# First loads on two queues, and GpSimd's start-up work in another order

## The chip, the cores and the metric

The kernel runs on one core of one Trainium2 chip. The metric is device time in microseconds (us) for one execution, the median of several runs. A profile of one further execution shows each engine's instructions: PE (TensorE matmul), PEld (its weight loads), DVE (VectorE), ACT (ScalarE), POOL (GpSimd) and SP (SyncE, which here only issues transfers). SPq, ACTq and so on are the engines' sequencers.

## What is computed

Linear attention with random features, and behind it a mixture of eight experts, each token going to one of them. Cut to what matters:

```python
q_s, k_s = q * D ** -0.25, k * D ** -0.25          # (8, 8, 576, 64) each
phi = lambda x: exp(h - max(h)) / sqrt(128)        # h = x @ omega.T - sum(x * x) / 2, omega is (128, 64)
q_p, k_p = phi(q_s), phi(k_s)
kv, z = einsum('bhsm,bhsd->bhmd', k_p, v), k_p.sum(axis=2)
x = (q_p @ kv) / (q_p @ z + 1e-6)                  # heads joined: 4608 rows of 512
logits = x @ w_gate                                # 8 experts
e = argmax(logits)                                 # gate weight: softmax(logits)[e]
out = gate * (relu(x @ w1[e]) @ w2[e])             # w1: 512 x 1024, w2: 1024 x 512
```

## The kernel before

**Units.** Attention is worked through in 72 units, nine for each of the eight batches: unit -1 takes the last 64 positions of all eight heads (the remainder), units 0 to 7 take 512 positions of one head. `run` walks over them as a software pipeline. In step i, PE turns the inputs of unit i+1 (`tr`, in PSUM) and DVE copies them to `th` (L157); PE multiplies `th` of unit i by the scaled omega (`pp`, L166) and DVE takes the maxima (`mx`, L172); ACT takes the exponentials `kp` of unit i and `qp` of unit i-1 (L180, four instructions each). Behind them come the turn of `qp`, the sums over `v` (`kf`, L206) and the outputs. `pp` has two PSUM buffers, so the product of a unit waits until the exponentials of the unit two before it are done. `tr`, `pt_om` and the turned `qp` share one PSUM buffer of tag "tt".

**Loads.** `load(b)` issues a batch's transfers: the remainders of k and q into `kqr` (two halves each, L111), the heads of k, q and v (L115), and the remainder of v into the zeroed buffers `rv` (two halves, L111). Batch 0 starts with single heads of k and q (128 KB), then come the gate weights into `G` (L124, two halves), then v for two heads, the remainder of v, and pairs of heads (256 KB each). All are issued by SP, in this order. Two copies of omega are loaded ahead of them (L75); PE turns them (L77) and ACT scales the result into `omt` (L79), which every `pp` needs.

**Counters.** The transfers that SP and ACT issue are counted on eight semaphores in turn (DMAHW0 to DMAHW7 in the rows of the built program). A transfer is issued only when the earlier ones on its semaphore have landed; that wait stands in the issuing engine's instruction stream. The recording layer sets each engine's order from the order of the code; between engines it decides which transfer comes next on the eight semaphores.

**Start-up.** GpSimd makes the identity, clears the gather buffers `xg` and `xgm` (L789), makes the routing's constants (`Routing.setup`, L406 to L454; DVE turns some of them into other types, L420 and L450 to L454), copies the identity into `G` (L89, 16 copies) and clears the four `rv` buffers (L95). The experts' phase follows attention and is not touched.

Of the kernel before, what the change touches and what calls it, by code (L numbers as in the profile page):

```python
# [8 lines left out]
F32 = mybir.dt.float32  # L9
F32R = mybir.dt.float32r  # L10
BF16 = mybir.dt.bfloat16
I32 = mybir.dt.int32
# [45 lines left out]
class Attention:  # L58
    def __init__(self, tc, ctx, ps, io, q, k, v, omega, wg, xs, routing, ident):
        self.tc, self.nc = tc, tc.nc  # L60
        self.q, self.k, self.v, self.xs, self.routing, self.ident = q, k, v, xs, routing, ident
        nc = tc.nc
        pool = lambda n, b, **kw: ctx.enter_context(tc.tile_pool(name=n, bufs=b, **kw))
        self.cp = pool("at_c", 1)
        self.io, self.ps = io, ps
        self.open = ExitStack()
        self.pp = self.open.enter_context(tc.tile_pool(name="ps_a", bufs=2, space=PSUM))
        self.tt = self.open.enter_context(tc.tile_pool(name="ps_t", bufs=1, space=PSUM))
        self.wk = pool("at_wk", 2)
        self.xo = pool("at_x", 2)  # L70
        cp = self.cp

        om = self.wk.tile([P, 2, D], F32, name="om", tag="kp")
        for i in range(2):
            nc.sync.dma_start(om[:, i, :], omega)  # L75
        pt = self.tt.tile([P, 2, 512], F32, name="pt_om", tag="tt")
        nc.tensor.transpose(pt[:, 0, :P], om.rearrange("p a d -> p (a d)"), ident)  # L77
        self.om = cp.tile([P, M], F32, name="omt")
        nc.scalar.mul(self.om, pt[:, 0, :P], SCALE)  # L79

        self.G = cp.tile([P, H, W - 1], F32, name="G")
        self.one = cp.tile([P, 1], F32, name="one")
        nc.gpsimd.memset(self.one, 1.0)
        self.eps = cp.tile([P, 1], F32, name="eps")
        nc.gpsimd.memset(self.eps, EPS)
        for a in range(2):
            r = slice(a * D, (a + 1) * D)
            for h in range(H):
                nc.gpsimd.tensor_copy(self.G[r, h, :D], ident[r, r])  # L89
        self.wg = wg  # L90


        self.rv = [[cp.tile([P, NP, D], F32, name=f"rv{i}{a}") for a in range(2)] for i in range(2)]
        for t in self.rv[0] + self.rv[1]:
            nc.gpsimd.memset(t, 0.0)  # L95
        self.st, self.last = {}, {}

    def load(self, b):
        nc, io = self.nc, self.io
        s = {}  # L100
        s["kqr"] = io.tile([P, 2, NP, D], F32, name=f"kqr_{b}", tag="kqr")
        for nm in "kq":
            s[nm] = io.tile([P, H, NJ, D], F32, name=f"{nm}_{b}", tag=nm)
        s["v"] = io.tile([P, H, NJ, D], F32, name=f"v_{b}", tag="v")
        s["vr"] = self.rv[b % 2]
        def rest(nms):
            for n, src in nms:
                rem = src[b, :, SM:, :].rearrange("(i a) p d -> a p i d", a=2)
                for a in range(2):
                    to = s["vr"][a] if n == 2 else s["kqr"][:, n]  # L110
                    nc.sync.dma_start(to[a * SR:(a + 1) * SR], rem[a])  # L111

        def main(nms, h):
            for nm, src in nms:
                nc.sync.dma_start(s[nm][:, h], src[b, h, :SM, :].rearrange("h (p j) d -> p h j d", j=NJ))  # L115

        kq, v = (("k", self.k), ("q", self.q)), (("v", self.v),)
        rest(((0, self.k), (1, self.q)))
        if b == 0:
            main(kq, slice(0, 1))  # L120
            main(kq, slice(1, 2))
            for a in range(2):
                with nc.allow_non_contiguous_dma(reason="gate weights"):
                    nc.sync.dma_start(self.G[a * D:(a + 1) * D, :, D:], self.wg.rearrange("(h d) e -> d h e", d=D))  # L124
            main(v, slice(0, 2))
        rest(((2, self.v),))
        for c in range(2 if b == 0 else 0, H, 2):
            main(kq + v, slice(c, c + 2))
        s["kva"] = self.xo.tile([P, H, W], F32, name=f"kva_{b}", tag="kva")
        s["x"] = self.xo.tile([P, NJ, H, D], F32, name=f"x_{b}", tag="x")  # L130
        s["xr"] = self.xo.tile([P, NP, D], F32, name=f"xr_{b}", tag="xr")
        s["lg"] = self.xo.tile([P, NJ, E], F32, name=f"lg_{b}", tag="lg")
        s["lgr"] = self.xo.tile([P, E, NP], F32, name=f"lgr_{b}", tag="lgr")
        self.st[b] = s
# [158 lines left out]
    def run(self, pre):  # L293
# [8 lines left out]
        for i in range(n):  # L302
# [30 lines left out]
                self.routing.row(2 if i % 4 == 0 else 1, self.nc.gpsimd)  # L333
            self.unit_sum(*u)
            pre.ahead(i - n)
            if u1:
                self.next = self.room(f"tr_{i}")
                self.routing.product(self.next[:, 1, 256:])
# [56 lines left out]
class Routing:  # L395
# [8 lines left out]
    def setup(self):  # L404
# [6 lines left out]
        self.RM = t("rt_RM", [P, NG, GT])  # L411
        self.RH = t("rt_RH", [P, NLT, 2, P], BF16)
        self.EX = t("rt_EX", [P, GT, E + 1])
        nc.gpsimd.memset(self.EX[:, :, E:], 1e-9)
        nc.gpsimd.memset(self.CU[:, 0, :], 0.0)

        self.iop = t("rt_iop", [P, P])
        self.iob = t("rt_iob", [P, P], BF16)
        nc.gpsimd.iota(self.iop, pattern=[[1, P]], base=0, channel_multiplier=0, allow_small_or_imprecise_dtypes=True)
        nc.vector.tensor_copy(self.iob, self.iop)  # L420
        self.rev = t("rt_rev", [P, E])
        nc.gpsimd.iota(self.rev, pattern=[[-1, E]], base=E, channel_multiplier=0, allow_small_or_imprecise_dtypes=True)
        self.zero = t("rt_zero", [P, P], BF16)
        nc.gpsimd.memset(self.zero, 0.0)
        self.ones = t("rt_ones", [P, P], BF16)
        nc.gpsimd.memset(self.ones, 1.0)
        self.tri = t("rt_tri", [P, P], BF16)
        nc.gpsimd.affine_select(out=self.tri, in_=self.ones, pattern=[[1, P]], compare_op=ALU.is_gt, fill=0.0,
                                base=0, channel_multiplier=-1)
        self.low = t("rt_low", [P, E, E])  # L430
        self.upp = t("rt_upp", [P, E, E])
        nc.gpsimd.memset(self.low, 1.0)
        nc.gpsimd.memset(self.upp, 1.0)
        nc.gpsimd.affine_select(out=self.low, in_=self.low, pattern=[[1, E], [-1, E]], compare_op=ALU.is_gt, fill=0.0,
                                base=0, channel_multiplier=0)
        nc.gpsimd.affine_select(out=self.upp, in_=self.upp, pattern=[[-1, E], [1, E]], compare_op=ALU.is_gt, fill=0.0,
                                base=0, channel_multiplier=0)
        self.fold = t("rt_fold", [P, SR])
        nc.gpsimd.tensor_copy(self.fold, ident[:, :SR])
        nc.gpsimd.tensor_tensor(out=self.fold, in0=self.fold, in1=ident[:, SR:], op=ALU.add)  # L440
        idi = t("rt_id", [P, NG, GT], I32)
        nc.gpsimd.iota(idi[:, :, :GT - 1], pattern=[[2 * S, NG], [S, 2], [1, NJ]], base=0, channel_multiplier=NJ)
        for a in range(2):
            nc.gpsimd.iota(idi[a * SR:(a + 1) * SR, :, GT - 1:], pattern=[[2 * S, NG]], base=SM + a * S,
                           channel_multiplier=1)
        part = t("rt_part", [P, NLT], I32)
        self.ihi = t("rt_ihi", [P, NLT])
        self.ilo = t("rt_ilo", [P, NLT])
        flat = idi.rearrange("p g s -> p (g s)")
        nc.vector.tensor_single_scalar(part, flat, 6, op=ALU.logical_shift_right)  # L450
        nc.vector.tensor_copy(self.ihi, part)
        nc.vector.tensor_scalar_add(self.ihi, self.ihi, -float(NT // 64))
        nc.vector.tensor_single_scalar(part, flat, 63, op=ALU.bitwise_and)
        nc.vector.tensor_copy(self.ilo, part)  # L454

    def open(self, ps, tag):
        self.ps, self.tag = ps, tag
# [313 lines left out]
class Experts:  # L771
# [6 lines left out]
    def __init__(self, tc, ctx, rt, xs, w1, w2, out, ident, ps):  # L778
# [6 lines left out]
        self.idx0 = cp.tile([P, 2], U32, name="idx0")  # L785
        self.flags = cp.tile([1, 5, NPR + 2], I32, name="flags")
        self.xg = [cp.tile([P, 2, ROW], F32, name=n) for n in ("xg", "xgm")]
        for x in self.xg:
            self.nc.gpsimd.memset(x, 0.0)  # L789
        rt.setup()  # L790
        *rt.after[3], last = rt.head(4, self.idx0, self.flags)
        rt.late[5] = [last]
# [327 lines left out]
def attention_moe(tc, q, k, v, omega, wg, w1, w2, out, xs):  # L1120
    nc = tc.nc
    with ExitStack() as ctx:
        cp = ctx.enter_context(tc.tile_pool(name="cp", bufs=1))
        ps = ctx.enter_context(tc.tile_pool(name="ps", bufs=1, space=PSUM))
        sched = lambda: tc.manual_schedule(engines={ET.PE, ET.Activation, ET.DVE, ET.Pool, ET.SP})
        ident = cp.tile([P, P], F32, name="ident")
        make_identity(nc, ident)
        rt = Routing(tc, ctx, xs, ident)
        ex = Experts(tc, ctx, rt, xs, w1, w2, out, ident, ps)
        with ExitStack() as c2:  # L1130
            io = c2.enter_context(tc.tile_pool(name="at_io", bufs=2))
            at = Attention(tc, c2, ps, io, q, k, v, omega, wg, xs, rt, ident)
            rt.open(ps, "nu")
            with sched():
                at.run(ex)
                ex.rest()
        with ExitStack() as c4:
            with sched():
                ex.run(c4, at.open.close)
# [23 lines left out]
```

## Time and profile before

| | us |
|---|---|
| median of three runs | 698.99 |
| lowest and highest | 698.91, 699.36 |
| the profiled execution, its own time | 701.15 |
| span of the profiled execution, first to last instruction | 699.3 |
| PE busy in the span | 672.8 |
| ACT busy | 359.9 |
| DVE busy | 372.6 |
| GpSimd busy | 272.4 |

The span is the part that the profile sees; 1.85 us of the profiled execution lie around it. Start times in rows count from the start of the span. A row of the timeline merges instructions that follow each other and are alike ("x4"), and a row with an engine's q at its end is an issue of a transfer; the transfer itself lands later, and the list of transfers gives the time from issue to landing. Idle time before an instruction stands in brackets with what ended it.

### The profile page before, as it was taken

To read this page: it belongs to the slowest core of one execution; us is meant where nothing else is said; L and a number is where in the kernel's file an instruction comes from. 1 tells how busy PE (TensorE), PEld (TensorE's weight loads), DVE (VectorE), ACT (ScalarE), POOL (GpSimd) and SP (SyncE) were. 2 spreads that over 40 slices of the span, in tenths; PEclk is the share of its full clock that TensorE was granted. 3 is DMA by queue.
4 is the path that set the end of the run, shared out by engine and by line. 5 is a ranking of instruction groups with operands and counts; after the bars stand their busy time and mean duration, and the time that the engine had idled before them with its cause. 6 is when DMAs were issued, how large, how long until landed. Compare 5 with 4: busy or idle time off the path is not lost. (4 is left out here: it accounts for less than half of the span.)

```text
span 699.3 us, 19723 instructions
## 1 busy us (share of the span) xinstructions
PE 672.8 (96%) x7596; PEld 615.6 (88%) x7596; DVE 372.6 (53%) x738; ACT 359.9 (51%) x1096; POOL 272.4 (39%) x484
## 2 busy tenths in 40 slices
PE   5999999999999999999999999999999999999992
PEld 4999999999898977899899988999898999998891
DVE  4788888888887778532222253422383365422220
ACT  3999999999998944322212262222262263222120
POOL 6455547886887763222112202222231132122020
PEclk9999999999999999999999999999999999999997
DMA  5953836628492124851233247332267338422200
GB/s 160 269 168 114 268 88 191 209 76 252 138 373 73 34 76 138 286 179 64 93 97 108 91 158 241 108 106 71 84 205 242 108 112 320 138 79 61 78 18 21
DMA packets 92432, 99.57 MB, mean 142 GB/s; under 512 B 28943, under 2 KB 72975, under 8 KB 91665
## 3 DMA queue, kind: packets, MB, share of 16 engines
q1 hardware_dynamic: 85744, 78.91, 35.9%
q0 software_dynamic: 6560, 19.03, 8.2%
q8 instruction: 72, 1.18, 0.7%
q14 instruction: 56, 0.45, 0.2%
HBM read 71.06 MB, written 29.51 MB: 144 GB/s over the span
## 5 line engine op out<-in xcount | busy, mean ns | idle before, releaser
L943 PEld LDWEIGHTS p<-xb,w1p 128*128 128x128 f32 x1632 | 198.1, 192 | 1.7 <-issue 0.5
L943 PE MATMUL p<-xb,w1p 128*128 128x256 f32 x1632 | 198.9, 283 | 0.0
L868 PE MATMUL p<-w2p,hh 128*128 128x512 f32 x576 | 177.8, 390 | 0.0
L1014 POOL DMA_INDIRECT out_dram<-ys,idx x38 | 39.4, 1038 | 313.4 <-ACT ys L1013 201.3
L868 PEld LDWEIGHTS p<-w2p,hh 128*128 128x128 f32 x576 | 107.0, 188 | 21.3
L868 PE MATMUL p<-w2p,hl 128*128 128x512 f32 x312 | 117.7, 389 | 0.0
L1013 ACT ACTIVATE ys<-p,gt 128x512 f32<-128x512 f32 x38 | 26.1, 688 | 163.2 <-PE p L868 146.2
L999 DVE SCALAR_TENSOR_TENSOR hl<-p,hh 128x512 fp32r<-128x512 f32 x68 | 46.0, 688 | 80.5 <-ACT hh L995 78.3
L995 ACT ACTIVATE hh<-p 128x512 fp32r<-128x512 f32 x68 | 39.9, 598 | 91.5 <-PE p L943 91.5
L172 DVE TENSOR_REDUCE mx<-pp 128x8 f32<-128x1024 f32 x64 | 78.0, 1218 | 11.4 <-PE pp L166 10.7
L180 ACT ACTIVATE qp<-pp,mx 128x128 f32<-128x128 f32 x256 | 77.4, 438 | 0.0
L180 ACT ACTIVATE kp<-pp,mx 128x128 f32<-128x128 f32 x256 | 74.2, 387 | 4.6 <-DVE de L264 1.1
L166 PE MATMUL pp<-omt,th 64*128 64x128 f32 x1024 | 73.4, 285 | 0.0
L868 PEld LDWEIGHTS p<-w2p,hl 128*128 128x128 f32 x312 | 58.5, 188 | 12.2
L166 PEld LDWEIGHTS pp<-omt,th 64*128 64x128 f32 x1024 | 64.8, 194 | 0.0
L192 POOL TENSOR_TENSOR k<-kp 128x256 f32<-128x256 f32 x64 | 46.6, 728 | 27.7 <-ACT kp L180 21.8
L157 DVE COPY th<-tr 128x512 f32<-128x512 f32 x63 | 43.3, 687 | 6.8 <-PE tr L151 4.8
L927 DVE STREAM_TRANSPOSE xgm<-xq 128x512 f32<-128x512 f32 x18 | 18.9, 1086 | 51.3 <-DMA xq<-pair_rows 51.3
L255 PE MATMUL nu<-kva,qt 128*64 128x73 f32 x1008 | 46.0, 233 | 0.0
L224 ACT COPY qt<-t 128x512 f32<-128x512 f32 x64 | 42.0, 656 | 3.1 <-PE t L151 2.5
L255 PEld LDWEIGHTS nu<-kva,qt 128*64 128x64 f32 x1008 | 36.7, 136 | 4.2
L206 PE MATMUL kf<-kp,v 128*64 128x128 f32 x512 | 39.4, 275 | 0.0
(365 smaller groups left out, 1002.0 us busy)
## 6 DMA issues: line engine op xcount, KB each, us to landing
w1s<-in_moe_w_dram SPq DMA_DIRECT2D x5, 2048.0 KB, 8.8
w2s<-in_moe_w_dram SPq DMA_DIRECT2D x5, 2048.0 KB, 11.0
xq<-pair_rows SPq DMA_DIRECT2D x76, 128.0 KB, 2.9
v<-in_v_dram SPq DMA_DIRECT2D x32, 256.0 KB, 6.4
token_rows<-x SPq DMA_DIRECT2D x8, 1024.0 KB, 8.0
k<-in_k_dram SPq DMA_DIRECT2D x31, 256.0 KB, 5.2
q<-in_q_dram SPq DMA_DIRECT2D x31, 256.0 KB, 5.9
pair_rows<-xg SPq DMA_DIRECT2D x10, 512.0 KB, 2.8
```

The lines of the kernel that those rows point to most:

```text
L157: self.nc.vector.tensor_copy(t.rearrange("p n (a t) -> p a n t", a=2), s[("tr", h)])
L166: nc.tensor.matmul(o[:, a, n, :], t[r, n, :], self.om[r], start=True, stop=True)
L172: self.nc.vector.tensor_reduce(out=mx, in_=s[("pp", h)], axis=AX.X, op=ALU.max, negate=True)
L180: self.nc.scalar.activation(o[:, j, :], p[:, a, 2 * n + i, :], AF.Exp, bias=mx[:, a, 2 * n + i:2 * n + i + 1])
L192: nc.gpsimd.tensor_tensor(out=k2, in0=kp[:, :2, :], in1=kp[:, 2:, :], op=ALU.add)
L206: nc.tensor.matmul(pkv[c * D:(c + 1) * D, :M], vv, kk, start=n < 2, stop=n > 2)
L224: self.nc.scalar.copy(qt.rearrange("p n (a t) -> p a n t", a=2), s[("t2", h)])
L255: nc.tensor.matmul(o[r, j, :], qt[:, j, r], kva[:, h if h >= 0 else 2 * j + a, :], start=True, stop=True)
L868: self.nc.tensor.matmul(p, x, w[:, c, :], start=c == 0 and x is h and w is self.w2h, stop=c == self.NF - 1 and x is l)
L943: return [lambda w=w, x=x, c=c, n=n: self.nc.tensor.matmul(o, w[:, c, f], x[:, c, :], start=n == 0, stop=n == len(ops) - 1) for n, (w, x, ...
L995: self.nc.scalar.activation(a, self.p_1[g], AF.Relu)
L999: self.nc.vector.scalar_tensor_tensor(out=b, in0=self.p_1[g], scalar=0.0, in1=a.bitcast(F32), op0=ALU.max, op1=ALU.subtract)
```

## The change

1. Of the first transfers, ACT now issues one copy of omega, the remainder of q, both halves of the gate weights, the first v and the remainder of v for batch 0. SP issues the rest. PE's turn of omega and ACT's scaling (`scaled`) are called from `load`, behind the issues of `kqr`.
2. GpSimd clears the four `rv` buffers ahead of the copies into `G`.
3. The routing's constants (`Routing.constants`) and the clearing of `xg` and `xgm` (`pre.clear`) are called at the end of step 0 of `run`. Attention is built within the hand-ordered stretch (`sched()`).

```diff
-        for i in range(2):
-            nc.sync.dma_start(om[:, i, :], omega)
-        pt = self.tt.tile([P, 2, 512], F32, name="pt_om", tag="tt")
-        nc.tensor.transpose(pt[:, 0, :P], om.rearrange("p a d -> p (a d)"), ident)
+        for i, eng in enumerate((nc.sync, nc.scalar)):
+            eng.dma_start(om[:, i, :], omega)
         self.om = cp.tile([P, M], F32, name="omt")
-        nc.scalar.mul(self.om, pt[:, 0, :P], SCALE)
+
+        def scaled():
+            pt = self.tt.tile([P, 2, 512], F32, name="pt_om", tag="tt")
+            nc.tensor.transpose(pt[:, 0, :P], om.rearrange("p a d -> p (a d)"), ident)
+            nc.scalar.mul(self.om, pt[:, 0, :P], SCALE)
+        self.scaled = scaled
...
+        for t in self.rv[0] + self.rv[1]:
+            nc.gpsimd.memset(t, 0.0)
         for a in range(2):
             r = slice(a * D, (a + 1) * D)
             for h in range(H):
                 nc.gpsimd.tensor_copy(self.G[r, h, :D], ident[r, r])
...
-                    nc.sync.dma_start(to[a * SR:(a + 1) * SR], rem[a])
+                    (nc.scalar if b == 0 and n else nc.sync).dma_start(to[a * SR:(a + 1) * SR], rem[a])
...
-                nc.sync.dma_start(s[nm][:, h], src[b, h, :SM, :].rearrange("h (p j) d -> p h j d", j=NJ))
+                (nc.scalar if b == 0 and nm == "v" and not h.start else nc.sync).dma_start(s[nm][:, h], src[b, h, :SM, :].rearrange("h (p j) d -> p h j d", j=NJ))
...
         if b == 0:
+            self.scaled()
             main(kq, slice(0, 1))
...
-                    nc.sync.dma_start(self.G[a * D:(a + 1) * D, :, D:], self.wg.rearrange("(h d) e -> d h e", d=D))
+                    nc.scalar.dma_start(self.G[a * D:(a + 1) * D, :, D:], self.wg.rearrange("(h d) e -> d h e", d=D))
...
             pre.ahead(i - n)
+            if i == 0:
+                self.routing.constants()
+                pre.clear()
...
-        for x in self.xg:
-            self.nc.gpsimd.memset(x, 0.0)
+        self.clear = lambda: [self.nc.gpsimd.memset(x, 0.0) for x in self.xg]
...
-            at = Attention(tc, c2, ps, io, q, k, v, omega, wg, xs, rt, ident)
-            rt.open(ps, "nu")
             with sched():
+                at = Attention(tc, c2, ps, io, q, k, v, omega, wg, xs, rt, ident)
+                rt.open(ps, "nu")
```

ACT's instructions at the start, before, with the semaphores that each waits for (`kp_-1` and `qp_-1` are the exponentials of unit -1, `kp_0` those of unit 0):

```order
L79 ACT_TABLE_LOAD
L79 ACTIVATE omt<-pt_om 128x128 [waits PE_49]
L180 ACTIVATE kp_-1_254<-pp_-1_242,mx_-1_251 128x128 [waits DVE_49]
L180 ACTIVATE kp_-1_254<-pp_-1_242,mx_-1_251 128x128 x3
L180 ACTIVATE qp_-1_308<-pp_-1_242,mx_-1_251 128x128 x4
```

And now:

```order
L75 DMA om<-in_omega_dram 128x64
L114 DMA kqr_162<-in_q_dram 64x4x64 x2
L81 ACT_TABLE_LOAD
L81 ACTIVATE omt<-pt_om 128x128 [waits PE_49]
L128 DMA G<-in_moe_w_gate_dram 64x8x8 [waits DMAHW1_49]
L128 DMA G<-in_moe_w_gate_dram 64x8x8 [waits DMAHW3_49]
L118 DMA v_165<-in_v_dram 128x2x256 [waits DMAHW5_49]
L114 DMA rv_138<-in_v_dram 64x4x64 [waits DMAHW7_49,Pool_49]
L114 DMA rv_139<-in_v_dram 64x4x64 [waits DMAHW1_49,Pool_49]
L184 ACTIVATE kp_-1_230<-pp_-1_218,mx_-1_227 128x128 [waits DVE_49]
L184 ACTIVATE kp_-1_230<-pp_-1_218,mx_-1_227 128x128 x3
L184 ACTIVATE qp_-1_308<-pp_-1_218,mx_-1_227 128x128 x4
```

Three issues now stand ahead of the table load, and five, each with a wait for a transfer semaphore, between `omt` and the first exponentials. SP's issues before, from the first head on:

```order
L115 DMA k_190<-in_k_dram 128x256
L115 DMA q_191<-in_q_dram 128x256
L115 DMA k_190<-in_k_dram 128x256 [waits DMAHW0_49]
L115 DMA q_191<-in_q_dram 128x256 [waits DMAHW1_49]
L124 DMA G<-in_moe_w_gate_dram 64x8x8 [waits DMAHW2_49]
L124 DMA G<-in_moe_w_gate_dram 64x8x8 [waits DMAHW3_49]
L115 DMA v_192<-in_v_dram 128x2x256 [waits DMAHW4_49]
L111 DMA rv_179<-in_v_dram 64x4x64 [waits DMAHW5_49,Pool_49]
L111 DMA rv_180<-in_v_dram 64x4x64 [waits DMAHW6_49,Pool_49]
L115 DMA k_190<-in_k_dram 128x2x256 [waits DMAHW7_49]
L115 DMA q_191<-in_q_dram 128x2x256 [waits DMAHW0_49]
```

And now, from the first head on:

```order
L118 DMA k_163<-in_k_dram 128x256
L118 DMA q_164<-in_q_dram 128x256
L118 DMA k_163<-in_k_dram 128x256 [waits DMAHW0_49]
L118 DMA q_164<-in_q_dram 128x256 [waits DMAHW1_49]
L118 DMA k_163<-in_k_dram 128x2x256 [waits DMAHW2_49]
L118 DMA q_164<-in_q_dram 128x2x256 [waits DMAHW3_49]
L118 DMA v_165<-in_v_dram 128x2x256 [waits DMAHW4_49]
L118 DMA k_163<-in_k_dram 128x2x256 [waits DMAHW5_49]
L118 DMA q_164<-in_q_dram 128x2x256 [waits DMAHW6_49]
L118 DMA v_165<-in_v_dram 128x2x256 [waits DMAHW7_49]
L118 DMA k_163<-in_k_dram 128x2x256 [waits DMAHW0_49]
```

The gate weights, the first v and the remainder of v are gone from SP's row, and the pairs of heads follow the single heads at once. DVE's first instructions before:

```order
L420 CAST rt_iob<-rt_iop 128x128
L450 TENSOR_SCALAR rt_part<-rt_id 128x36
L451 CAST rt_ihi<-rt_part 128x36
L452 TENSOR_SCALAR rt_ihi<-rt_ihi 128x36
L453 TENSOR_SCALAR rt_part<-rt_id 128x36
L454 CAST rt_ilo<-rt_part 128x36
L157 COPY th_-1_229<-tr_first 128x2x4x64
L157 COPY th_0_240<-tr_second 128x2x4x64
L172 TENSOR_REDUCE mx_-1_251<-pp_-1_242 128x8
L157 COPY th_1_295<-tr_259 128x2x4x64
```

And now:

```order
L161 COPY th_-1_205<-tr_first 128x2x4x64
L161 COPY th_0_216<-tr_second 128x2x4x64
L176 TENSOR_REDUCE mx_-1_227<-pp_-1_218 128x8
L440 CAST rt_iob<-rt_iop 128x128
L459 TENSOR_SCALAR rt_part<-rt_id 128x36
L460 CAST rt_ihi<-rt_part 128x36
L461 TENSOR_SCALAR rt_ihi<-rt_ihi 128x36
L462 TENSOR_SCALAR rt_part<-rt_id 128x36
L463 CAST rt_ilo<-rt_part 128x36
L161 COPY th_1_295<-tr_259 128x2x4x64
```

The six instructions on the routing's constants now stand between the maxima of unit -1 and the copy of unit 1's turned inputs.

## Rows read from the trace of the kernel before

**Rows 1.** The page, part 1: busy us, share of the span, instructions.

```profile
PE 672.8 (96%) x7596; PEld 615.6 (88%) x7596; DVE 372.6 (53%) x738; ACT 359.9 (51%) x1096; POOL 272.4 (39%) x484
```

**Rows 2.** Busy time of each engine by stretch, granted clock, DMA share, GB/s.

```profile
4.00:8.00 4.00, 1.69 (x10) 0.98 (x10) 1.90 (x7) 0.12 (x1) 3.83 (x23) 1.00 0.66 172
18.00:20.00 2.00, 2.00 (x22) 1.67 (x20) 0.78 (x2) 1.73 (x8) 0.51 (x1) 1.00 1.09 343
20.00:24.00 4.00, 4.00 (x82) 3.82 (x82) 2.59 (x4) 2.97 (x12) 1.61 (x4) 1.00 0.89 200
20.00:240.00 220.00, 216.30 (x4533) 203.50 (x4532) 183.11 (x397) 211.59 (x809) 147.87 (x291) 1.00 0.57 174
```

**Rows 3.** The timeline of PE: start, us, instruction, idle time before it.

```profile
6.70 0.47 PE L151 MATMUL tr_first<-ident,kqr 64*128 64x64 f32 x3 [0.83 <-DMA kqr<-in_q_dram]
...
14.61 0.48 PE L151 MATMUL tr<-ident,q 64*128 64x64 f32 x4 [0.36 <-DMA q<-in_q_dram]
14.88 2.02 PE L166 MATMUL pp<-omt,th 64*128 64x128 f32 x16
```

**Rows 4.** Weight loads of the products L166 in two stretches: duration ns min/median/max.

```profile
L166 PEld LDWEIGHTS pp<-omt,th x32: 330/330/335, 10.6 to 16.3; 64*128 64x128 f32 x32
...
L166 PEld LDWEIGHTS pp<-omt,th x176: 188/188/194, 22.2 to 57.8; 64*128 64x128 f32 x176
```

**Rows 5.** The timeline of SP: start and duration of the issues.

```profile
0.81 0.89 SPq L75 DMA_DIRECT2D om<-in_omega_dram  x2
1.74 1.41 SPq L111 DMA_DIRECT2D kqr<-in_k_dram  x2
3.20 1.27 SPq L111 DMA_DIRECT2D kqr<-in_q_dram  x2
4.51 0.60 SPq L115 DMA_DIRECT2D k<-in_k_dram  x1
...
9.21 1.29 SPq L111 DMA_DIRECT2D rv<-in_v_dram  x2
10.56 0.60 SPq L115 DMA_DIRECT2D k<-in_k_dram  x1
...
14.79 0.53 SPq L115 DMA_DIRECT2D v<-in_v_dram  x1
...
20.84 0.97 SPq L115 DMA_DIRECT2D k<-in_k_dram  x1
22.03 0.37 SPq L115 DMA_DIRECT2D q<-in_q_dram  x1
```

**Rows 6.** Transfers issued at 4.51, 10.56 and 14.79: KB, us from issue to landing.

```profile
k<-in_k_dram SPq DMA_DIRECT2D x1, 128.0 KB, 2.6
...
k<-in_k_dram SPq DMA_DIRECT2D x1, 256.0 KB, 3.1
...
v<-in_v_dram SPq DMA_DIRECT2D x1, 256.0 KB, 7.2
```

**Rows 7.** The timeline of ACT: the table load and the exponentials of unit -1.

```profile
0.81 1.28 ACT L79 ACT_TABLE_LOAD   x1 [0.81 <-PEq L1150]
...
11.77 1.14 ACT L180 ACTIVATE kp_-1_254<-pp_-1_242,mx_-1_251 128x128 f32<-128x128 f32 x4 [7.64 <-DVE mx_-1_251 L172]
12.78 1.16 ACT L180 ACTIVATE qp_-1_308<-pp_-1_242,mx_-1_251 128x128 f32<-128x128 f32 x4
```

**Rows 8.** The timelines of DVE and GpSimd: constants, maxima of unit -1, last clears.

```profile
3.48 0.61 DVE L420 CAST rt_iob<-rt_iop 128x128 bf16<-128x128 f32 x1 [3.48 <-POOL rt_iop L419]
5.42 0.20 DVE L450 TENSOR_SCALAR rt_part<-rt_id 128x36 int32<-128x36 int32 x1 [1.33 <-POOL rt_id L444]
...
6.46 0.18 DVE L454 CAST rt_ilo<-rt_part 128x36 f32<-128x36 int32 x1
...
10.51 1.23 DVE L172 TENSOR_REDUCE mx_-1_251<-pp_-1_242 128x8 f32<-128x1024 f32 x1 [1.13 <-PE pp_-1_242 L166]
...
8.87 1.07 POOL L95 MEMSET rv<- 128x256 f32 x4
```

More of the change, by code (lines that the diff above doesn't have):

```diff
@@ L85, in __init__ @@
         nc.gpsimd.memset(self.eps, EPS)
+        self.wg = wg
+        self.rv = [[cp.tile([P, NP, D], F32, name=f"rv{i}{a}") for a in range(2)] for i in range(2)]
+        for t in self.rv[0] + self.rv[1]:
+            nc.gpsimd.memset(t, 0.0)
         for a in range(2):
@@ L89, in __init__ @@
                 nc.gpsimd.tensor_copy(self.G[r, h, :D], ident[r, r])
[L90 to L95, printed above, removed]
         self.st, self.last = {}, {}
@@ L413, in setup, with constants @@
         self.EX = t("rt_EX", [P, GT, E + 1])
+        self.iop = t("rt_iop", [P, P])
+        self.iob = t("rt_iob", [P, P], BF16)
+        self.rev = t("rt_rev", [P, E])
+        self.zero = t("rt_zero", [P, P], BF16)
+        self.ones = t("rt_ones", [P, P], BF16)
+        self.tri = t("rt_tri", [P, P], BF16)
+        self.low = t("rt_low", [P, E, E])
+        self.upp = t("rt_upp", [P, E, E])
+        self.fold = t("rt_fold", [P, SR])
+        self.idi = t("rt_id", [P, NG, GT], I32)
+        self.part = t("rt_part", [P, NLT], I32)
+        self.ihi = t("rt_ihi", [P, NLT])
+        self.ilo = t("rt_ilo", [P, NLT])
+    def constants(self):
+        nc, ident = self.nc, self.ident
         nc.gpsimd.memset(self.EX[:, :, E:], 1e-9)
         nc.gpsimd.memset(self.CU[:, 0, :], 0.0)
-        self.iop = t("rt_iop", [P, P])
-        self.iob = t("rt_iob", [P, P], BF16)
         nc.gpsimd.iota(self.iop, pattern=[[1, P]], base=0, channel_multiplier=0, allow_small_or_imprecise_dtypes=True)
         nc.vector.tensor_copy(self.iob, self.iop)
-        self.rev = t("rt_rev", [P, E])
         nc.gpsimd.iota(self.rev, pattern=[[-1, E]], base=E, channel_multiplier=0, allow_small_or_imprecise_dtypes=True)
-        self.zero = t("rt_zero", [P, P], BF16)
         nc.gpsimd.memset(self.zero, 0.0)
-        self.ones = t("rt_ones", [P, P], BF16)
         nc.gpsimd.memset(self.ones, 1.0)
-        self.tri = t("rt_tri", [P, P], BF16)
         nc.gpsimd.affine_select(out=self.tri, in_=self.ones, pattern=[[1, P]], compare_op=ALU.is_gt, fill=0.0,
                                 base=0, channel_multiplier=-1)
-        self.low = t("rt_low", [P, E, E])
-        self.upp = t("rt_upp", [P, E, E])
         nc.gpsimd.memset(self.low, 1.0)
@@ L437, in setup @@
                                 base=0, channel_multiplier=0)
-        self.fold = t("rt_fold", [P, SR])
         nc.gpsimd.tensor_copy(self.fold, ident[:, :SR])
         nc.gpsimd.tensor_tensor(out=self.fold, in0=self.fold, in1=ident[:, SR:], op=ALU.add)
-        idi = t("rt_id", [P, NG, GT], I32)
-        nc.gpsimd.iota(idi[:, :, :GT - 1], pattern=[[2 * S, NG], [S, 2], [1, NJ]], base=0, channel_multiplier=NJ)
+        nc.gpsimd.iota(self.idi[:, :, :GT - 1], pattern=[[2 * S, NG], [S, 2], [1, NJ]], base=0, channel_multiplier=NJ)
         for a in range(2):
-            nc.gpsimd.iota(idi[a * SR:(a + 1) * SR, :, GT - 1:], pattern=[[2 * S, NG]], base=SM + a * S,
+            nc.gpsimd.iota(self.idi[a * SR:(a + 1) * SR, :, GT - 1:], pattern=[[2 * S, NG]], base=SM + a * S,
                            channel_multiplier=1)
[L446 to L451, printed above, removed]
+        flat = self.idi.rearrange("p g s -> p (g s)")
+        nc.vector.tensor_single_scalar(self.part, flat, 6, op=ALU.logical_shift_right)
+        nc.vector.tensor_copy(self.ihi, self.part)
         nc.vector.tensor_scalar_add(self.ihi, self.ihi, -float(NT // 64))
-        nc.vector.tensor_single_scalar(part, flat, 63, op=ALU.bitwise_and)
-        nc.vector.tensor_copy(self.ilo, part)
+        nc.vector.tensor_single_scalar(self.part, flat, 63, op=ALU.bitwise_and)
+        nc.vector.tensor_copy(self.ilo, self.part)
     def open(self, ps, tag):
```

## The prediction

> **What bounds the kernel now.** I read the page's part 1 first: PE is busy for 96% of the span [rows 1]. The windows say where it is not. From 20 to 240 us, the rest of attention, PE is busy for 216.3 of 220 us [rows 2], so nearly every microsecond that the start gains or loses is still there at the end. Only the start itself has holes. The mark by which I measure it is the first product that is followed by work without a break, `pp` of unit 1, which starts on PE at 14.88, after a turn that waited for a load of q until 14.61 [rows 3]. A change that moves this product by some time moves the end by the same time, unless something else comes last.
>
> Two levels of PE's clock lie in this stretch. The granted clock reads 1.00 in every window [rows 2], yet the weight loads of the same products take 330 ns up to 16 us and 188 ns from 22 us on [rows 4]: 1.2 GHz first, 2.4 GHz later, and the rise came some 6 us after PE's last wait. I take it that the rise moves with the work. If it comes a microsecond earlier or later than that, half of the PE work in that microsecond is won or lost, 0.5 us at most, and this goes into the range.
>
> **Where the loads stand.** SP issues without a break from 0.81 to about 9 us, then the remainder of v waits for GpSimd's clears, and the pair of heads that PE waits for goes out at 10.56 only [rows 5]. It lands 3.1 us later [rows 6], at 13.7. In the stretch from 4 to 8 us the DMA engines are busy for 0.66 of the time at 172 GB/s, against 343 GB/s from 18 to 20 us [rows 2]: at first the issues are the limit, not the transfers.
>
> **What sharing the queues wins.** SP loses one copy of omega (half of 0.89, so 0.45 us) and the remainder of q (1.27 us and a gap of 0.04) [rows 5]. The first head of k goes out at 4.51 - 1.77 = 2.74 and lands 2.6 us later [rows 6], at 5.34. ACT issues the remainder of q from 1.28 on, where SP issued it from 3.20 on: 1.92 us earlier. The turn of the remainder, whose last part waited for that load and ended at 7.17 [rows 3], would end at 5.25, if the table load is not late. That load now stands behind three issues: 0.81 + 0.45 + 1.31 = 2.57, and 1.28 us of loading [rows 7] end at 3.9, early enough for `omt` at about 4.2. The maxima of unit -1 start at 10.51 [rows 8] and would then start at about 8.7 and end at 9.9.
>
> **What the constants cost.** On DVE they now stand behind these maxima: 0.61 us for the first and 1.22 us from 5.42 to 6.64 for the other five [rows 8], so 1.83 us. They would end at 11.7, the copy of unit 1 at 12.4, and its product could start at 12.85. GpSimd's start-up work, which ended at 9.94 [rows 8], is the same in another order, with the clears of `xg` last; what DVE needs is made by then. If nothing else came last, the product would start 2.0 us earlier than at 14.88. Without DVE's wait for room behind the maxima it would be up to 1.83 us more; so much this step costs in that case, and nothing where PE is held by something later.
>
> **What the moved issues cost.** ACT now issues five transfers between `omt` and the exponentials of unit -1, and each has a wait for one of the eight semaphores in turn. Such a wait is in the rows of before: SP was free at 21.81, yet issued a load of q at 22.03 [rows 5], just after the load of v issued at 14.79 had landed, 7.2 us later, at 22.0 [rows 6]. The two have nothing in common but the semaphore. In the changed program the remainder of v on ACT waits for DMAHW7 to count two loads, and the two before it there are the first q and the third pair of v, the sixth pair of heads on SP. The first v on ACT waits in the same way for the second pair of k. ACT works its row in order, so the exponentials of unit -1 queue behind the landing of a load that is not needed before unit 4.
>
> When does that sixth pair land? From the first k's landing at 5.34, three single heads and six pairs follow, 7.5 pairs in all. In the trace nine pairs in a row landed from 13.66 to 21.99 [rows 5, 6], eight steps of 1.04 us. So 7.5 x 1.04 = 7.8 us, at 13.1. The gate weights and the first v come in between on the other queue; I add 0.3 us for them, an estimate, and take 13.4. The bounds are the rates of two stretches: a pair is 262,144 bytes, 0.76 us at 343 GB/s and 1.31 us at 200 GB/s [rows 2], so 11.1 and 15.2. Then two issues with their waits, 1.29 us on SP [rows 5], and the exponentials of unit -1 start at 14.7 (12.4 to 16.5) instead of 11.77 [rows 7]. No row shows an issue on ACT; on SP one took 0.45 us to 0.97 us [rows 5], so the pair lies between 0.9 and 1.94 us. I keep 1.29, since the transfers are the same.
>
> `pp` has two buffers, so unit 1's product waits for the last exponential of unit -1. From the first to the last that is 13.94 - 11.77 = 2.17 us [rows 7]. The product starts at 14.7 + 2.17 = 16.9, against 14.88 [rows 3]: 2.0 us later. The constants on DVE, done at 11.7, and the clears on GpSimd lie under this wait and cost nothing.
>
> **The sum.** On the profiled execution the span becomes 699.3 + 2.0 = 701.3 us, its own time 701.15 + 2.0 = 703.2. Its time lies 2.2 us above the median of the runs, 698.99; on the median the sum is 701.0 us. By the bounds of the landing the shift lies between -0.3 and +3.8 us, so 698.7 to 702.8.
>
> Whether the wait holds ACT's engine or the transfer alone, rows show for SP alone. Here the Trainium skill speaks against the change: "DMA: Bandwidth & Descriptors", section "Anatomy of one DMA — SWDGE (gpsimd) path", says that the DMA engines wait for no semaphore, and that the wait happens on the issuing sequencer before dispatch. By that the exponentials are held and the sum is 701.0; with a wait beside the engine it would be that of the second rival, 697.0. SP's issue at 22.03 agrees with the page; no run here shows it for ACT.
>
> **The rivals.**
> - The same wait, but the loads land faster than 1.04 us a pair. At 343 GB/s [rows 2] the exponentials start at 12.4 and the product at 14.6; the change is then worth -0.3 us, and anything up to +1.4 us can't be told from no change. For it speaks that the rate rose to 343 GB/s; against it that this was one stretch of 2 us, and that a second queue now takes a share. Time: 699.7, the middle between 698.7 and 700.4.
> - Faster: ACT is through with its issues before the maxima of unit -1 are ready at 9.9. Then the product starts at 12.85, 2.0 us earlier, 697.0 us. The point is the landing of the sixth pair: at 8.6 the exponentials aren't held at all, at 11.4 the change breaks even. Against it: from 5.34 to 8.6 there would be 0.43 us for a pair, 600 GB/s, which no row has. So it needs ACT not to be held by the waits.
> - The change doesn't do what it says: the loads of two queues land no earlier than those of one. The Trainium skill has a rule to that effect ("DMA: Bandwidth & Descriptors", "Issuing engines are not separate DMA queues": all run on the same 16 engines, and only issue time is saved). As a mechanism of this kernel it means that the maxima of unit -1 still end at 11.74 and, with 1.83 us of constants, unit 1's product could start at 14.7, as before: 699.0 us if ACT isn't held. The window from 4 to 8 us with 0.66 of the DMA time in use [rows 2] speaks against it.
>
> **How the numbers follow.** Forecast (held by about 2 us) 0.68; faster landing 0.20; not held 0.08; nothing gained or lost 0.04. The likeliest gives 701.0. The range leaves out the third case and little of the others: 699.0 to 703.0, the upper end from the bound of 702.8 and slower issues on ACT. A measurement of this kernel can tell about 0.2%, 1.4 us, from no change. Slower by more than that 0.69, within it 0.23, faster 0.08.
>
> **What would show it.** In the profile after, the row of ACT shows the issues of the remainder of v at about 13.4, with nothing done in between, and the exponentials of unit -1 at about 14.7; idle time of the exponentials is put down to a DMA or to ACT's own queue. DVE's maxima of unit -1 end near 10 and its constants near 12. PE waits some 3 us ahead of unit 1's product, for ACT and no longer for a load. The forecast is wrong if the exponentials of unit -1 start before 12.7, or if the product of unit 1 starts late and PE makes it good before 240 us.

## The result, and the profile after

The changed kernel takes 703.19 us (median of six runs, 702.36 to 704.8), the kernel before beside it 698.96 (six runs, 698.9 to 699.36): ratio 1.0062, interval 1.005 to 1.0073. A second comparison (below) gives 703.45 against 699.66. The direction was forecast, the size was not: 4.2 and 3.8 us instead of 2.0.

| | before | after |
|---|---|---|
| profiled execution, its own time | 701.15 | 704.8 |
| its span | 699.3 | 702.9 |
| first product followed by unbroken work (`pp` of unit 1) | 14.88 | 17.88 |
| exponentials of unit -1 start | 11.77 | 15.65 |

Part 1 of the page, answering to [rows 1]: no engine does more work than before.

```profile
PE 671.9 (96%) x7596; PEld 615.2 (88%) x7596; DVE 371.7 (53%) x738; ACT 359.8 (51%) x1096; POOL 272.4 (39%) x484
```

The windows of after, with the columns of [rows 2] (PE, PEld, DVE, ACT, POOL busy, granted clock, DMA share, GB/s):

```profile
4.00:8.00 4.00, 2.23 (x22) 1.88 (x24) 1.16 (x2) 0.25 (x1) 3.78 (x23) 1.00 0.81 218
14.00:16.00 2.00, 0.00 (x0) 0.00 (x0) 0.00 (x0) 0.35 (x2) 0.00 (x0) 0.59 1.14 263
18.00:20.00 2.00, 2.00 (x22) 2.00 (x24) 0.00 (x0) 1.89 (x8) 0.98 (x2) 0.50 0.39 88
20.00:24.00 4.00, 4.00 (x67) 3.62 (x63) 2.88 (x3) 3.25 (x11) 1.94 (x5) 0.85 0.79 218
20.00:240.00 220.00, 216.16 (x4520) 203.35 (x4518) 183.85 (x397) 212.00 (x808) 148.35 (x292) 1.00 0.56 172
240.00:260.00 20.00, 18.13 (x224) 15.33 (x221) 13.37 (x54) 8.42 (x32) 12.57 (x24) 0.91 0.25 84
```

From 4 to 8 us the DMA engines do more than before (0.81 against 0.66), so the two queues do what they are for. From 14 to 16 us every engine except ACT is empty. From 20 to 240 us PE is as busy as before: what the start lost is not made good there. The granted clock, 1.00 in every window of [rows 2], now falls twice: once in the gap (0.59 from 14 to 16 us, 0.50 from 18 to 20, 0.85 from 20 to 24) and once from 240 to 260 us (0.91).

The timeline of PE, answering to [rows 3]: the turn of the remainder, of unit 1 (9.30), of unit 2 (12.36), which PE does ahead of unit 1's product, and that product.

```profile
5.33 0.68 PE L155 MATMUL tr_first<-ident,kqr 64*128 64x64 f32 x7 [0.67 <-DMA kqr<-in_k_dram]
...
9.30 0.42 PE L155 MATMUL tr<-ident,q 64*128 64x64 f32 x4
...
12.36 0.29 PE L155 MATMUL tr<-ident,q 64*128 64x64 f32 x4
17.88 2.08 PE L170 MATMUL pp<-omt,th 64*128 64x128 f32 x16 [5.22 <-ACT qp_-1_308 L184]
```

Unit 2's inputs are turned by 12.65, 2.4 us before those of [rows 3]. The turn of q takes 0.29 us, the one before it, at 9.30, still took 0.42: PE had risen to 2.4 GHz, some 8 us sooner than before. Then PE waits 5.22 us, and no longer for a load but for ACT. The timeline of ACT, answering to [rows 7], says why ("ACTq" is an issue of a transfer, and a row of "x2" reaches from the first issue to the end of the second):

```profile
2.68 1.28 ACT L81 ACT_TABLE_LOAD   x1 [2.68 <-issue]
3.97 0.28 ACT L81 ACTIVATE omt<-pt_om 128x128 f32<-128x128 f32 x1
7.24 4.28 ACTq L128 DMA_DIRECT2D G<-in_moe_w_gate_dram  x2
12.39 0.39 ACTq L118 DMA_DIRECT2D v<-in_v_dram  x1
14.30 1.31 ACTq L114 DMA_DIRECT2D rv<-in_v_dram  x2
15.65 1.14 ACT L184 ACTIVATE kp_-1_230<-pp_-1_218,mx_-1_227 128x128 f32<-128x128 f32 x4 [11.40 <-DMA G<-in_moe_w_gate_dram]
16.66 1.16 ACT L184 ACTIVATE qp_-1_308<-pp_-1_218,mx_-1_227 128x128 f32<-128x128 f32 x4
```

Between 4.25 and 15.65 ACT computes nothing. Each issue waits for an earlier transfer of SP's on its semaphore, so its start tells by when that one had landed: the second q by 7.24, the second pair by 10.92 (the second issue of `G`, the end of its row less 0.60), the fourth by 12.39, the sixth by 14.30. (A pair is a load of two heads, counted in SP's order.) The list of transfers, which gave the landings of [rows 6], has none for after; these issues stand in for them. The profile puts the exponentials' idle time down to the load of `G`, one of the waits behind which they stood.

SP and DVE, answering to [rows 5] and [rows 8]:

```profile
2.96 0.63 SPq L118 DMA_DIRECT2D k<-in_k_dram  x1
...
5.05 0.43 SPq L118 DMA_DIRECT2D k<-in_k_dram  x1
...
7.58 0.47 SPq L118 DMA_DIRECT2D v<-in_v_dram  x1
```

```profile
9.35 1.23 DVE L176 TENSOR_REDUCE mx_-1_227<-pp_-1_218 128x8 f32<-128x1024 f32 x1 [1.13 <-PE pp_-1_218 L170]
10.49 0.22 DVE L440 CAST rt_iob<-rt_iop 128x128 bf16<-128x128 f32 x1
...
11.45 0.68 DVE L161 COPY th<-tr 128x512 f32<-128x512 f32 x1
```

SP issues the first head of k at 2.96 instead of 4.51, and the sixth pair at 7.58. The maxima of unit -1 end at 10.6, 1.2 us before those of [rows 8], and ACT could have started then. Weight loads of the products in two stretches, answering to [rows 4]:

```profile
L170 PEld LDWEIGHTS pp<-omt,th x16: 284/330/330, 17.9 to 19.3; 64*128 64x128 f32 x16
...
L170 PEld LDWEIGHTS pp<-omt,th x186: 188/188/194, 21.9 to 60.0; 64*128 64x128 f32 x186
```

Behind the wait, PE works at 1.2 GHz again, as it did in this place before: the gap took back the early rise of the clock.

### The profile page after: what moved, and what is told of

It reads as the page before. It is cut to its first block, busy times and chain, and to the rows that moved or that the text cites. A ratio compares the mean times of both kernels' runs of the same rounds, so it can differ in the third digit from the quotient of the medians.

```text
span 702.9 us, 19718 instructions
## 1 busy us (share of the span) xinstructions
PE 671.9 (96%) x7596; PEld 615.2 (88%) x7596; DVE 371.7 (53%) x738; ACT 359.8 (51%) x1096; POOL 272.4 (39%) x484
```

## The experiments

The theory is that of the forecast: ACT's last issues wait for late pairs of heads, and the exponentials of unit -1 queue behind them (the hold). Rival one: two queues are slower as such. Rival two: the constants, now behind the first maxima, cost the time. Line numbers are those of the changed kernel.

**Two kernels that keep the queues and take the hold away.** The first leaves only one copy of omega and the remainder of q on ACT:

```diff
-  (nc.scalar if b == 0 and n else nc.sync).dma_start(to[...], rem[a])
+  (nc.scalar if b == 0 and n == 1 else nc.sync).dma_start(to[...], rem[a])
-  (nc.scalar if b == 0 and nm == "v" and not h.start else nc.sync).dma_start(s[nm][:, h], ...)
+  nc.sync.dma_start(s[nm][:, h], ...)
-  nc.scalar.dma_start(self.G[...], ...)
+  nc.sync.dma_start(self.G[...], ...)
```

> The changed kernel, but ACT issues only the copy of omega and the remainder of q; the gate weights, the first v and the remainder of v are SP's again, at their old place. Theory (the exponentials of unit -1 are held behind ACT's issues, which wait for loads of later heads): nothing holds ACT, the exponentials of unit -1 start near 10.5 us and the product of unit 1 near 12.7 us, so the time is 2.2 us under the kernel before, about 696.8 us. Rival one (loading over two queues makes the loads late in itself): still 701 us or more. Rival two (the routing's constants behind the first maxima cost the time): about 703 us, since they stand where they stood.

The second has the first line of that diff alone: the gate weights and the first v stay on ACT, and only the remainder of v goes to SP. In its built program ACT's waits are for the first k, the first q and the second q.

> The changed kernel, but the remainder of v is issued by SP ahead of the pairs of heads; ACT still issues the gate weights and the first v. In the built program ACT's issues then wait for single heads alone (the last for the second q). Theory: the last of these waits ends at about 7.3 us, before the first maxima are done, so the exponentials of unit -1 start near 10.5 us and the time is about 696.8 us, though ACT issues six of its eight transfers. Rival one (two queues as such): 701 us or more. Rival two (constants): about 703 us.

The first: 697.9 against 700.24, ratio 0.9962 (0.9944 to 0.998); the recorded ratios are not exactly the quotients of the two medians. The second: 698.67, ratio 0.9975 (0.9963 to 0.9987). The product of unit 1 in the first, and then ACT and PE of the second:

```profile
12.90 1.11 PE L170 MATMUL pp<-omt,th 64*128 64x128 f32 x16
```

```profile
5.72 1.32 ACTq L128 DMA_DIRECT2D G<-in_moe_w_gate_dram  x2
7.31 0.46 ACTq L118 DMA_DIRECT2D v<-in_v_dram  x1
10.50 1.14 ACT L184 ACTIVATE kp_-1_230<-pp_-1_218,mx_-1_227 128x128 f32<-128x128 f32 x4 [6.25 <-DMA G<-in_moe_w_gate_dram]
```

```profile
12.72 2.08 PE L170 MATMUL pp<-omt,th 64*128 64x128 f32 x16
```

Three late issues still stand in ACT's row here, but what they wait for has landed by 7.31. The exponentials start when the maxima are done, and the product of unit 1 at 12.72, 5.2 us ahead of the changed kernel's. So it is in the first, at 12.90. It is not the second queue, nor the issues, nor the constants, which stand in both kernels where the change put them. Rivals one and two fall as causes of the loss.

**Only the order of GpSimd's work and the constants,** all loads on SP:

```diff
-  for i, eng in enumerate((nc.sync, nc.scalar)):
+  for i, eng in enumerate((nc.sync, nc.sync)):
...
-  (nc.scalar if b == 0 and n else nc.sync).dma_start(to[...], rem[a])
+  nc.sync.dma_start(to[...], rem[a])
...
```

> The changed kernel with all loads issued by SP, so only GpSimd's order and the place of the routing's constants differ from the kernel before. Theory: the pair of heads goes out about 1 us earlier since the clears of the remainder of v are done, the constants take about 1.1 us on DVE behind the first maxima, and the product of unit 1 starts near 13.8 us: 697.9 us, 1.1 us under the kernel before. Rival two (the constants cost the time): 702 us or more. Rival one: no more than the kernel before, 699 us.

699.64, ratio 1.0004 (0.9988 to 1.002; the two medians alone would give 0.9991): by itself this part neither costs nor gains anything that can be told. The expected 697.9 and 13.8 us were missed: its product of unit 1 starts at 14.59, behind a wait of 0.93 for q, so the loads are again what comes last.

**Does the granted clock of 0.50 behind the gap cost?** Fourteen products on a zero tile fill a part of PE's wait:

```diff
+            if i == 2:
+                self.routing.warm(self.ps.tile([P, 512], F32, name="hot", tag="kf"), 14)
```

> The changed kernel, with 14 products of zeros on PE in the gap in which it waits for the exponentials of unit -1, ahead of the product of unit 1. The hold stays as it is. If the fall of the granted clock in that gap (0.50 in the changed kernel's trace from 16 to 20 us) is part of the price, the clock stays at 1.00 and the time falls by about 1.5 us to 701.7 us. If the clock plays no part, the time stays at 703.2 us or rises a little.

703.72, ratio 1.0048 (1.0023 to 1.0073), against 1.0052 for the changed kernel in its second comparison. The product of unit 1 now runs at 2.4 GHz:

```profile
18.79 1.16 PE L170 MATMUL pp<-omt,th 64*128 64x128 f32 x16 [1.21 <-ACT qp_-1_308 L184]
```

It takes 1.16 us instead of 2.08, but in this execution the hold lasted 0.9 us longer (18.79 against 17.88), and the time is the same. The experiment doesn't price the clock; it shows only that it isn't what made the kernel slower.

**The size again, and the hold made shorter and longer.** First the changed kernel unchanged.

> The changed kernel once more, for its size beside the kernel before, whose runs spread from 698.5 to 702.7 us. Theory (ACT held by the wait of its last issues): exponentials of unit -1 at 15.65 and the product of unit 1 at 17.9 again, 3.0 us later than before; against a kernel before of 700.2 the median is then 703.2, ratio 1.0043, and of the 4.2 us about 1.2 was the luck of the first runs of before. If instead the fall of the clock at 250 us belongs to the change, the profile shows it again and the ratio is 1.006. Rival (two queues as such, or the constants): says nothing else here.

703.45 against 699.66, ratio 1.0052 (1.0034 to 1.007). Its ACT and PE:

```profile
8.04 3.56 ACTq L128 DMA_DIRECT2D G<-in_moe_w_gate_dram  x2
12.48 0.39 ACTq L118 DMA_DIRECT2D v<-in_v_dram  x1
14.24 1.98 ACTq L114 DMA_DIRECT2D rv<-in_v_dram  x2
16.27 1.14 ACT L184 ACTIVATE kp_-1_230<-pp_-1_218,mx_-1_227 128x128 f32<-128x128 f32 x4 [12.02 <-DMA v<-in_v_dram]
```

```profile
18.50 2.08 PE L170 MATMUL pp<-omt,th 64*128 64x128 f32 x16 [5.83 <-ACT qp_-1_308 L184]
```

The sixth pair landed at 14.24 as in the first execution, yet the exponentials start 0.6 us later: the second `rv` issue came at 15.62 (the row's end less 0.60). Its transfer semaphore, DMAHW1, counts one copy of omega, the second q (landed by 8.04) and the first load of `G`, which ACT itself had issued at 8.04; so `G` is what it waited for, though the profile puts ACT's idle time down to v.

Then the gate weights back on SP, so that ACT's last issue waits for the third pair instead of the sixth:

```diff
-  nc.scalar.dma_start(self.G[a * D:(a + 1) * D, :, D:], ...)
+  nc.sync.dma_start(self.G[a * D:(a + 1) * D, :, D:], ...)
```

> The gate weights go back to SP, so that ACT keeps the remainder of q, the first v and the remainder of v; its last issue then waits for the third pair of heads (first pair of v) and no longer for the sixth. Theory: the third pair lands at about 12.0, the exponentials of unit -1 start at about 12.7, the product of unit 1 at 14.9 as in the kernel before, and the time is that of before, 700.2 (ratio 1.000, 0.998 to 1.002). Rival one (a second queue slows the loads as such): three transfers of the first v and the remainder of v still stand on ACT's queue, so 703. Rival two (constants behind the maxima): they stand there as in the changed kernel, so 703.

702.03, ratio 1.0028 (1.0014 to 1.0042). The hold is shorter, but not as short as I expected:

```profile
9.29 4.68 ACTq L114 DMA_DIRECT2D rv<-in_v_dram  x2
14.02 1.14 ACT L184 ACTIVATE kp_-1_230<-pp_-1_218,mx_-1_227 128x128 f32<-128x128 f32 x4 [9.76 <-DVE th L161]
```

```profile
16.25 2.08 PE L170 MATMUL pp<-omt,th 64*128 64x128 f32 x16 [3.36 <-ACT qp_-1_308 L184]
```

The first `rv` went out at 9.29 when the first pair had landed, the second at 13.37 (4.68 - 0.60 behind it) when the third had: 2.04 us a pair. In that time ACT's queue moved 0.26 MB, its v, and SP's queue 0.85 MB, where two pairs are 0.52 MB: the pairs shared the engines with loads issued behind them. The expectation of no change is refuted; the order of the kernels is not.

Then the queues alone, GpSimd's order and the constants as in the kernel before; here ACT's last waits are for the seventh pair and for its own `G`:

```diff
-            if i == 0:
-                self.routing.constants()
-                pre.clear()
```

(`constants` is called in `setup`, the clears of `xg` and of `rv` stand where they stood before.)

> Only the first part of the change: the two queues. GpSimd's order, the constants and the clears are as in the kernel before. In the built program the last issues of ACT now wait for the seventh pair instead of the sixth. Theory: a pair more, 1.1 us: exponentials of unit -1 at 16.8, product of unit 1 at 19.0, 1.1 us above the changed kernel, 704.3 (ratio 1.006). Rival two (the constants on DVE between the maxima and the copy cost the time): 1.05 us of DVE are gone from there, so 702.2 or less. Rival one: as the changed kernel, 703.2.

704.74, ratio 1.0069 (1.0046 to 1.0092). The median is what was expected, but its profiled execution (702.91, the lowest of six) doesn't show the longer hold:

```profile
14.42 1.37 ACTq L114 DMA_DIRECT2D rv<-in_v_dram  x2
15.83 1.14 ACT L184 ACTIVATE kp_-1_254<-pp_-1_242,mx_-1_251 128x128 f32<-128x128 f32 x4 [11.59 <-DMA G<-in_moe_w_gate_dram]
```

15.83 instead of 16.8. So what remains is that taking the constants from behind the maxima wins nothing under the hold, as the forecast said.

**A kernel that beats both (sorted loads).** Loads as in the first kernel, the first pair of k and q ahead of v and the gate weights, and DVE's six instructions in step 3:

```diff
+            main(kq, slice(2, 4))
             main(v, slice(0, 2))
...
+            if i == 3:
+                self.routing.converted()
```

> Only one copy of omega and the remainder of q on ACT; on SP the first pair of k and q stands ahead of the first v, its remainder and the gate weights; DVE's six instructions on the constants run in step 3 instead of step 0. Theory: nothing holds ACT; exponentials of unit -1 at 10.5, product of unit 1 at 12.7 without a wait for q, that of unit 2 at 15.7 instead of 16.2: 697.4 (ratio 0.996). Rival two: if the constants were what cost the time, more is won, 1.05 us against the kernel with the late loads back on SP: 696.8. Rival one has no price here.

698.7 against 699.66, ratio 0.9978 (0.9965 to 0.9991). The product of unit 1 starts at 12.77 and that of unit 2 at 15.73, as expected, but the time is not the expected 697.4 and not better than the first kernel's, which was run again:

> The kernel with only one copy of omega and the remainder of q on ACT, once more on its own, since it and the one with its loads sorted further came out at ratios of 0.9962 and 0.9978 beside different runs of the kernel before. Theory: product of unit 1 at 12.9, about 1.9 us ahead of the kernel before, and a ratio of 0.997 with an interval below 1. Rival: the gain was one of the chip of that call; the interval takes in 1.

698.32 against 700.12, ratio 0.9974 (0.9964 to 0.9984), product of unit 1 at 12.74. So about 2 us can be won with the two queues, and the two moves of the kernel with sorted loads add nothing that can be told.

**The kernel before, profiled three times more.** In the later comparisons its runs spread over 3 to 5 us (697.56 to 702.72 in all).

> The kernel before, profiled once more. The forecast measured every shift against one profiled execution, whose time (701.15) lies above the middle of all runs of before (700.0 of 48). Theory: that execution has a slower start than most (the clock rose at 20.2 us); another one shows the product of unit 1 at about 14.3 instead of 14.88 or an earlier rise of the clock, and unit 3's exponentials about 1 us earlier. Rival: the start is the same in every execution (14.9, rise at 20.2), and the spread of before comes from behind 240 us.

> As the one before it: theory 14.3 and an earlier rise of the clock, rival 14.9 and 20.2 us.

> As the two before it: theory 14.3 and an earlier rise of the clock, rival 14.9 and 20.2 us.

700.57, 700.28 and 701.75. The product of unit 1 in the three:

```profile
14.72 2.02 PE L166 MATMUL pp<-omt,th 64*128 64x128 f32 x16
```

```profile
14.71 2.02 PE L166 MATMUL pp<-omt,th 64*128 64x128 f32 x16
```

```profile
15.01 2.02 PE L166 MATMUL pp<-omt,th 64*128 64x128 f32 x16
```

The theory of a slow start in one execution falls: all four start alike, and the weight loads of all four come down from 330 to 188 ns between 20.0 and 20.6 us. But the third has a window that no part of the change can have made:

```profile
240.00:260.00 20.00, 18.40 (x183) 15.46 (x180) 14.73 (x57) 8.51 (x30) 13.82 (x23) 0.91 0.25 76
```

The same granted clock of 0.91 from 240 to 260 us stood in the first profile of the changed kernel. Its second profile has 1.00 there, and the kernel with sorted loads, which is faster, 0.91 again. That fall comes and goes from one execution to the next.

**All kernels in a row,** by the product of unit 1 in the profile, beside the median less that of the kernel before in the same comparison:

| kernel | product of unit 1, us | median, us against before |
|---|---|---|
| remainder of v on SP | 12.72 | -1.57 |
| remainder of q alone on ACT, two comparisons | 12.90, 12.74 | -2.34, -1.80 |
| sorted loads | 12.77 | -0.96 |
| all loads on SP | 14.59 | -0.60 |
| before | 14.71 to 15.01 | 0 |
| gate weights on SP | 16.25 | +2.37 |
| changed kernel, two comparisons | 17.88, 18.50 | +4.23, +3.79 |
| queues alone | 18.06 | +5.08 |
| changed kernel, products of zeros in the gap | 18.79 | +3.48 |

The four medians without a hold have a mean of -1.67 at 12.78, the four with the long hold one of +4.15 at 18.31: 5.8 us of time for 5.5 us of this product, about one for one, with a scatter of about 1 us between kernels. What the kernels without a hold win in their profiles is more than this product shows, because their clock also rises earlier: the exponentials of unit 2 start 3.3 to 4.0 us ahead of those of before, the product of unit 1 only 1.9 to 2.1.

## Why the forecast was right in direction and short in size

**The mechanism was right.** ACT's exponentials stood behind issues, an issue behind a semaphore that it shared with a load needed much later, and taking that wait away turned +4 us into some -2 us. The Trainium skill ("DMA: Bandwidth & Descriptors", section "Anatomy of one DMA — SWDGE (gpsimd) path") says that the wait is on the issuing sequencer; ACT's idle 11.40 us agree, here for an issue from ACT.

**The gain ahead of the hold was right to some 0.6 us.** The first k was to go out at 2.74 and went at 2.96; the table load was to end at 3.9 and ended at 3.96. The turn of the remainder ended at 6.0, not at 5.25, because its last part now waited for the remainder of k. The constants were to end at 11.7 and ended at 11.54, by two errors against each other: they began later, and took 1.05 us instead of 1.83 (`rt_iob` 0.22 us instead of 0.61). The kernel without late issues has its product of unit 1 at 12.90 where I had written 12.85; that it is so close is in part luck, since it rests on the same two errors. The rival "nothing gained" falls with it. The Trainium skill's rule that several issuing engines save only issue time, "usually small relative to the DMA itself" ("DMA: Bandwidth & Descriptors", "Issuing engines are not separate DMA queues"), holds in kind: the first k went out 1.55 us earlier. Together with the other two parts of the change, which alone gave nothing that can be told, that was worth 1.8 and 2.3 us.

**The first step that failed is the landing of the sixth pair.** I put it at 13.4: 7.5 pairs at 1.04 us each behind the first k, and 0.3 us for the gate weights and the first v. It landed at 14.30. So the exponentials started at 15.65 instead of 14.7 and the product at 17.88 instead of 16.9. The steps behind it held: 1.31 us for the two issues (forecast 1.29), 2.23 us from the exponentials to the product (2.17). What SP's queue (q1) moved tells more. The changed kernel's first profile, from the start to 14.30 and from 5.34 to 14.30 us, then the kernel before from 13.66 to 21.99 us, the stretch from which I took the rate (packets, MB, share of the 16 engines):

```profile
q1 hardware_dynamic: 3435, 2.79, 66.2%
```

```profile
q1 hardware_dynamic: 2520, 2.41, 87.8%
```

```profile
q1 hardware_dynamic: 3434, 2.26, 97.6%
```

The rate was no slower: 2.41 MB in 8.96 us and 2.26 MB in 8.33 us are both 0.97 us for the 262,144 bytes of a pair. But SP's loads up to and with the sixth pair are 2.26 MB, and 2.79 MB had moved when it landed. The other 0.53 MB, as much as two pairs, belong to loads that SP issued behind it, from 8.09 on (2.83 MB by 14.24 in the second profile). My sum let the queue finish one load after the other and counted only what stands ahead of the sixth pair. Why the landing lies behind the bytes, no run shows. ACT's queue moved 0.02 MB from 5.34 to 14.30, so the 0.3 us for the gate weights and the first v stood for transfers that had hardly begun.

**A second term was missing.** ACT's last issue waits for `G` as well, by the built program, and I put that wait at nothing and priced only the pair. In the second execution `G` came last, at 15.62, and the exponentials at 16.27.

**Part of this came back by the clock.** I allowed 0.5 us for the rise of the clock; it gave back about 1.0. In before PE works at 1.2 GHz for 5.4 us from this product on (14.83, the mean of the four, to 20.3). In after it is 3.3 us, from 17.88 to 21.2: a granted clock of 0.85 from 20 to 24 us is 1.2 us at 0.50 and 2.8 us at 1.00. That is 2.1 us less at half the speed. So the lag behind the mean of the four profiles of before shrinks: at the product of unit 1 it is 3.05 us in the first profile and 3.67 in the second, at the start of unit 2's exponentials 2.1 and 2.9, and at the end of attention 2.5 and 2.7, where I had 2.0. In profiled executions the miss is thus 0.5 to 0.7 us up to there, and my 703.2 for the profiled time stands against 704.8 (with the fall of the clock at 250 us) and 703.45 (without).

**The second step that failed is the way from the profile to the median.** I took 2.2 us off, since the one profiled execution of before lay that far above its three runs. The two profiles of after lie only 1.6 and 0.0 us above their medians. The four profiles of before have a mean of 700.9, and each lies above the median of all 70 runs of before beside these kernels, 699.87. With this base and the lag at the end of attention, 699.87 + 2.6 = 702.5; with the 1.1 us by which the profiled executions of before are slow among its runs, 703.5, against the changed kernel's 703.19 and 703.45. The kernels without a hold show the same offset from the other side: their four profiled executions lie 3.1 us below the mean of before's, their medians only 1.67 below those of before. This is arithmetic, not a cause: why the profiled executions of before are slower than most of its others, no run shows. Three of the four have a mean granted clock of 0.993, the others mostly 0.990 or 0.991, so the clock takes another course in them; where, a run without a profile doesn't tell. This stays open.

Two slips in the working cost nothing: the shortest issue of SP in [rows 5] is 0.37 us, not 0.45, and the middle between 698.7 and 700.4 is 699.55, not 699.7.

## What to carry to other kernels

An issue on a compute engine is an instruction in its row: before moving one there, look up in the built program which earlier transfer it waits for, and ask when that lands, not when the moved transfer is needed. Move the issues whose waits are over by then (here the remainder of q), and leave the others on the queue that computes nothing. When adding up when a load lands, allow for the loads issued behind it: here the sixth pair landed when the bytes of two more pairs had moved. And before a shift read from one profiled execution is set on a median, profile the kernel before several times: here four executions lay on average 1.1 us above the median of its runs, not 2.2.

## What the runs showed that I had not expected

**A small transfer on an idle queue didn't start for 3 us.** The first half of the gate weights (16 KB) was issued on ACT's queue at 7.24. Packets by queue in the changed kernel's first profile (queue, packets, MB, share of the 16 engines; q1 is SP's queue, q10 ACT's), from 7.2 to 10.5 us and from 10.5 to 12.5 us:

```profile
q1 hardware_dynamic: 868, 0.83, 79.6%
```

```profile
q1 hardware_dynamic: 631, 0.61, 89.7%
q10 hardware_dynamic: 453, 0.01, 12.8%
```

In the first stretch not one packet of ACT's queue moved, while SP's queue, with up to eight loads waiting in it, moved 868. The Trainium skill ("DMA: Bandwidth & Descriptors", "Queues, rings and completion order") says that a DMA engine takes its rows in turn, packet by packet; by that some of these would have moved early. Here they didn't, and no run shows why. It was not one execution's chance: in the second profile no packet of ACT's queue moved from the issue at 8.04 to 12.0 us, and with the gate weights back on SP ACT's v, issued at 7.91, moved none before 10.0.

**The granted clock fell in a gap and once more far behind it.** In the changed kernel PE waited 5.2 us, and the clock granted was 0.50 from 18 to 20 us, while it worked again. Shorter waits could do it too: the kernel with all loads on SP, whose PE waited 1.26 and 0.93 us for k and q, had 0.69 from 14 to 16 us. The fall to 0.91 in the window from 240 to 260 us follows a wait of PE of 1.5 to 1.7 us at the end of attention, which all fourteen profiles have. But it came in only four of the thirteen after the first one of before: the first of the changed kernel, one of before, the one with the gate weights on SP and the one with sorted loads.
